# Group normalisation of 128 images: the loads of scale and offset move from SP's DMA queue to ACT's

## Chip, cores and metric

The kernel runs on one core of a Trainium2 chip. The metric is the device time of one execution in microseconds, lower being better. The time before is the median of three runs.

## The reference

```python
# x: (128, 1024, 32, 16), g and b: (1024,), all bfloat16
def reference(x, g, b):
    G = 32
    B, C, H, W = x.shape
    xr = x.reshape(B, G, C // G, H, W)
    mu = xr.mean(axis=(2, 3, 4), keepdims=True)
    var = ((xr - mu) ** 2).mean(axis=(2, 3, 4), keepdims=True)
    xn = (xr - mu) / jnp.sqrt(var + 1e-5)
    xn = xn.reshape(B, C, H, W)
    return xn * g[None, :, None, None] + b[None, :, None, None]
```

Each of 128 x 32 groups (32 channels of 512 elements, 16384 values) is normalised by its own mean and variance, and each channel is then scaled by g and shifted by b.

## The kernel before

One partition holds one group: a tile is 4 images x 32 groups = 128 partitions with 16384 bfloat16 values each, 4 MB. There are 32 tiles (NT) in 6 buffers (SLOTS). A tile is loaded into its buffer, worked on in place and stored from it.

Everything is in hand-written order with semaphores; no scheduler moves anything. Each engine has its own list of instructions.

- **SP** issues the loads (`load`, L136 to L140) on its DMA queue. Before load i it waits until the store that last used the buffer has landed, so the first six loads go without a wait, and load 6 waits for store 0. Between load 0 and load 1 it issues the loads of scale and offset (L151, L152) into `gam_b` and `bet_b`, 128 partitions with 32 values of 2 bytes. The access pattern of their source, `four`, repeats the 32 rows of g or b four times: its outer dimension is 4 with step 0. Both loads count up the semaphore `s_gb`.
- **PE** sums 16 blocks of 512 columns of the tile into PSUM with the unit matrix as weights (`sums`, L198).
- **ACT** loads its function table and runs a small square root to warm up (L182). Per tile it computes the sum of squares in two parts (`squares`, L222), then issues the store of the tile before (`stored()`, in the end L143 and L144), then waits for DVE's variance (L231) and takes the square root (L232). The first store also waits until load 3 has landed (L344). All stores are on ACT's DMA queue.
- **DVE** sets two constants, then waits for both loads of scale and offset (L183) and converts them to float32 (L184, L185). Per tile (`normalise`) it sums the rest of the columns (L243), adds PE's sums (L253), forms the mean (L263), the deviation of the shift used in the squares (L272), waits for ACT's squares (L281), forms the variance (L285), waits for ACT's root, takes the reciprocal (L294), forms the 32 scales and offsets (L296, L300) and scales the tile in place, one instruction of 512 columns for each of 32 channels (L310).
- **POOL** prepares the unit matrix.

Of the kernel before, what the change touches and what calls it, by code (L numbers as in the profile page):

```python
# [24 lines left out]
def kernel(  # L25
# [37 lines left out]
    g_v = g.rearrange("(q k) -> q k", q=G)  # L63
    b_v = b.rearrange("(q k) -> q k", q=G)
# [5 lines left out]
    def sb(name, shape, dtype):  # L70
        return ctx.enter_context(nc.sbuf_tensor(name, shape, dtype))
# [3 lines left out]
    def sem(name):  # L75
        all_sems.append(nc.alloc_semaphore(name))
        return all_sems[-1]
# [7 lines left out]
    gam_b = sb("gam_b", [P, KC], BF16)  # L85
    bet_b = sb("bet_b", [P, KC], BF16)
# [38 lines left out]
    s_gb = sem("gb")  # L125
# [8 lines left out]
    sp, pe, act, dve, pool = nc.sync, nc.tensor, nc.scalar, nc.vector, nc.gpsimd  # L134

    def load(i):  # L136
        j, n = (i + FIRST) % SLOTS, i // SLOTS
        if n > 0:
            sp.wait_ge(s_store[j], 16 * n)
        sp.dma_start(out=xs[j][:], in_=x_v[i]).then_inc(s_load[j], 16)  # L140
# [5 lines left out]
    def four(v):  # L146
        return bass.AP(tensor=v.tensor, offset=v.offset, ap=[[0, NS]] + list(v.ap))


    load(0)  # L150
    sp.dma_start(out=gam_b[:], in_=four(g_v)).then_inc(s_gb, 16)  # L151
    sp.dma_start(out=bet_b[:], in_=four(b_v)).then_inc(s_gb, 16)  # L152
    for i in range(1, NT):
        load(i)
    for j in range(SLOTS):
# [7 lines left out]
        out=half[:],  # L163
        in_=ones[:],
# [8 lines left out]
        out=eye[:],  # L173
        in_=half[:],
# [3 lines left out]
        base=0,  # L178
        channel_multiplier=-1,
    ).then_inc(s_eye, 1)  # L180
    act.wait_ge(s_eps, 1)
    act.activation(out=warm[:], in_=eps_t[:], func=ACT.Sqrt)  # L182
    dve.wait_ge(s_gb, 32)  # L183
# [7 lines left out]
        out=ps[0][:, 0:P], lhsT=eye[:], rhs=eye[:], start=True, stop=True  # L191
# [215 lines left out]
```

## Time and profile before

| | before |
|---|---|
| median of three runs | 630.02 us (629.59 to 630.5) |
| the profiled execution | 630.21 us |
| its span | 628.5 us |
| DVE busy | 539.9 us (86%) |
| ACT busy | 471.2 us (75%) |
| PE busy | 185.0 us (29%) |
| moved by DMA | 268.48 MB, 427 GB/s on average |
| SP's DMA queue (q1) | 4872 packets, 134.24 MB |
| ACT's DMA queue (q10) | 4608 packets, 134.22 MB |

The span is the profiled execution from its first to its last instruction; the device time is 1.7 us longer. Busy times are of one engine; the engines work side by side. The two DMA queues are lists that the same 16 DMA engines work off. The page counts packets, one contiguous piece of a transfer each: 32 KB for a partition of x, 64 bytes for a partition of scale or offset, 4 bytes for the write to a semaphore that ends an engine's share of a transfer.

### The profile page before, as it was taken

What the parts mean: (1) busy time and instruction counts of PE and PEld (TensorE: products, weight loads), DVE (VectorE), ACT (ScalarE), POOL (GpSimd) and SP (SyncE); (2) the same over time, 40 slices, a digit from 0 to 9 for tenths busy, and PEclk for the clock granted to TensorE, in tenths of its full rate; (3) what the DMA queues carried; (4) which work ended last, traced back from release to release, by engine and by line L of the source; (5) the groups of instructions that cost most, each with busy time, mean ns of one, the idle gap of its engine ahead of it and who ended that gap; (6) DMA issues with size and microseconds to landing.
All of it is one profiled execution on the core that took longest, in us unless ns stands there. A gap on an engine that the chain in (4) does not pass through costs nothing.

```text
span 628.5 us, 2380 instructions
## 1 busy us (share of the span) xinstructions
PE 185.0 (29%) x508; PEld 0.1 (0%) x1; DVE 539.9 (86%) x1380; ACT 471.2 (75%) x162; POOL 0.8 (0%) x6
## 2 busy tenths in 40 slices
PE   1655214321333312343113332133330234312300
PEld 0000000000000000000000000000000000000000
DVE  0587999999999999999999988889888898888970
ACT  2977888888889888888879777797676886768800
POOL 0000000000000000000000000000000000000000
PEclk9767666656676567666666766677656766566655
DMA  9999999999999999999999999999999999999997
GB/s 368 429 434 422 428 411 434 434 434 434 432 434 434 434 434 434 430 434 434 432 434 434 432 434 434 434 434 432 432 434 434 434 432 430 432 432 434 432 434 309
DMA packets 9483, 268.48 MB, mean 427 GB/s; under 512 B 1288, under 2 KB 1288, under 8 KB 1288
## 3 DMA queue, kind: packets, MB, share of 16 engines
q1 hardware_dynamic: 4872, 134.24, 49.8%
q10 hardware_dynamic: 4608, 134.22, 49.5%
q14 instruction: 3, 0.02, 0.0%
HBM read 134.23 MB, written 134.22 MB: 427 GB/s over the span
## 4 chain that ended last, share of the span: by engine, by line
another core or an unknown queue 42%; DVE 30%; DMA 18%; SPq 2%; issue 2%; ACT 2%; ACTq 1%; DVEq 0%
DVE x L310 20%; DMA x<-in_x_dram 10%; DMA out_dram<-x 8%; DVE jp L243 7%; SPq L140 2%; ACT js L222 1%; DVE jd L253 1%; ACTq L144 1%; ACT scalars L232 1%; DVE bia L300 1%; DVE scl L296 0%; DVE scalars L285 0%; DVE scalars L263 0%; DVE scalars L272 0%
## 5 line engine op out<-in xcount | busy, mean ns | idle before, releaser
L222 ACT ACTIVATE js<-x 128x8192 uint8<-128x8192 bf16 x64 | 455.6, 7119 | 69.6 <-DMA x<-in_x_dram 67.9
L310 DVE TENSOR_SCALAR x<-x,scl,bia 128x512 bf16<-128x512 bf16 x1024 | 333.6, 406 | 1.2
L198 PE MATMUL ps<-x,eye 128*128 128x512 bf16 x507 | 184.7, 541 | 402.6 <-DMA x<-in_x_dram 401.5
L243 DVE SCALAR_TENSOR_TENSOR jp<-x 128x4096 uint8<-128x4096 bf16 x32 | 141.3, 4416 | 1.1 <-issue 1.1
L232 ACT ACTIVATE scalars<-scalars,eps_t 128x1 f32<-128x1 f32 x32 | 9.4, 294 | 56.7 <-DVE scalars L285 49.5
L281 DVE TENSOR_TENSOR scalars<-scalars 128x1 f32<-128x1 f32 x32 | 4.9, 154 | 32.1 <-ACT js L222 32.0
L253 DVE TENSOR_SCALAR_CACHE_REDUCE jd<-ps 128x512 f32<-128x512 f32 x32 | 22.2, 693 | 0.0
L294 DVE RECIPROCAL scalars<-scalars 128x1 f32<-128x1 f32 x32 | 5.2, 164 | 16.0 <-ACT scalars L232 16.0
L222 ACT ACTIVATION_READ_ACCUMULATOR js<-x 128x1 f32 x64 | 11.9, 186 | 0.0
L184 DVE CAST gam<-gam_b 128x32 f32<-128x32 bf16 x1 | 0.2, 182 | 12.5 <-DMA bet_b<-in_b_dram 12.5
L300 DVE SCALAR_TENSOR_TENSOR bia<-scl,scalars,bet 128x32 f32<-128x32 f32 x32 | 8.1, 252 | 1.1
L296 DVE TENSOR_SCALAR scl<-gam,scalars 128x32 f32<-128x32 f32 x32 | 7.7, 242 | 1.1
L272 DVE TENSOR_SCALAR scalars<-x,scalars 128x1 f32<-128x1 bf16 x32 | 6.9, 214 | 1.4 <-DVE scalars L263 0.3
L285 DVE SCALAR_TENSOR_TENSOR scalars<-scalars 128x1 f32<-128x1 f32 x32 | 7.0, 219 | 1.1
L263 DVE TENSOR_SCALAR scalars<-scalars 128x1 f32<-128x1 f32 x32 | 6.9, 214 | 1.1
L253 DVE DVE_READ_ACCUMULATOR jd<-ps 128x1 f32 x32 | 4.5, 139 | 0.0
L243 DVE DVE_READ_ACCUMULATOR jp<-x 128x1 f32 x32 | 2.6, 81 | 0.0
L182 ACT ACT_TABLE_LOAD x1 | 1.3, 1283 | 1.0 <-ACTq L66 1.0
L159 DVE MEMSET eps_t<- 128x1 f32 x1 | 0.1, 59 | 1.1 <-ACTq L66 1.1
L190 PE MATMUL ps<-eye 128*128 128x128 bf16 x1 | 0.3, 287 | 2.1 <-POOL eye L172 2.1
L162 POOL TENSOR_SCALAR_AFFINE_SELECT half<-ones 128x128 bf16<-128x128 bf16 x1 | 0.3, 292 | 0.9 <-DVE ones L160 0.9
L172 POOL TENSOR_SCALAR_AFFINE_SELECT eye<-half 128x128 bf16<-128x128 bf16 x1 | 0.3, 292 | 0.1
(8 smaller groups left out, 1.0 us busy)
## 6 DMA issues: line engine op xcount, KB each, us to landing
x<-in_x_dram SPq DMA_DIRECT2D x32, 4096.0 KB, 26.3
out_dram<-x ACTq DMA_DIRECT2D x32, 4096.0 KB, 50.4
gam_b<-in_g_dram SPq DMA_DIRECT2D x1, 8.0 KB
bet_b<-in_b_dram SPq DMA_DIRECT2D x1, 8.0 KB
```

Source lines behind the costliest of these rows:

```text
L140: sp.dma_start(out=xs[j][:], in_=x_v[i]).then_inc(s_load[j], 16)
L198: m = pe.add_instruction(mybir.InstMatmult(name=nc.get_next_instruction_name(), ins=[pe.lower_ap(xs[j][:, k * MM_FREE : (k + 1) * MM_FREE] ...
L222: act.activation(out=js[:, 0 : part.shape[1]], in_=part, func=ACT.Square, bias=xs[j][:, 0:1], scale=-1.0, accum_out=sq[j][:, k : k + 1],). ...
L232: act.activation(out=std[j][:], in_=nvar[j][:], func=ACT.Sqrt, bias=eps_t[:], scale=-inv_n,).then_inc(s_std[j], 1)
L243: dve.scalar_tensor_tensor(out=jp[:], in0=xs[j][:, PE_COLS : PE_COLS + PAIRS], scalar=1.0, in1=xs[j][:, PE_COLS + PAIRS : F], op0=ALU.mult ...
L253: dve.tensor_scalar(out=jd[:], in0=ps[j][:], scalar1=1.0, scalar2=None, op0=ALU.mult, op1=ALU.add, accum_out=sum1[j][:],).then_inc(s_sums[ ...
L263: dve.tensor_scalar(out=negmean[j][:], in0=sum1[j][:], scalar1=sum2[j][:], scalar2=-inv_n, op0=ALU.add, op1=ALU.mult,).then_inc(s_mean[j], 1)
L272: dve.tensor_scalar(out=d[j][:], in0=xs[j][:, 0:1], scalar1=negmean[j][:], scalar2=float(ROOT), op0=ALU.add, op1=ALU.mult,)
L285: dve.scalar_tensor_tensor(out=nvar[j][:], in0=d[j][:], scalar=d[j][:], in1=sqsum[j][:], op0=ALU.mult, op1=ALU.subtract,).then_inc(s_nvar[ ...
L296: dve.tensor_scalar(out=scl[j][:], in0=gam[:], scalar1=rstd[j][:], scalar2=None, op0=ALU.mult).then_inc(s_scl[j], 1)
L300: dve.scalar_tensor_tensor(out=bia[j][:], in0=scl[j][:], scalar=negmean[j][:], in1=bet[:], op0=ALU.mult, op1=ALU.add,).then_inc(s_bia[j], 1)
L310: v = dve.tensor_scalar(out=xs[j][:, k * HW : (k + 1) * HW], in0=xs[j][:, k * HW : (k + 1) * HW], scalar1=scl[j][:, k : k + 1], scalar2=bi ...
```

## The change

The two DMA issues for scale and offset are taken from SP's list, where they stood between load 0 and load 1, and put on ACT's list ahead of the function table load and the warm-up. Their source, destination and semaphore stay the same, and so does every wait.

```diff
     load(0)
-    sp.dma_start(out=gam_b[:], in_=four(g_v)).then_inc(s_gb, 16)
-    sp.dma_start(out=bet_b[:], in_=four(b_v)).then_inc(s_gb, 16)
     for i in range(1, NT):
         load(i)
...
+    act.dma_start(out=gam_b[:], in_=four(g_v)).then_inc(s_gb, 16)
+    act.dma_start(out=bet_b[:], in_=four(b_v)).then_inc(s_gb, 16)
     act.wait_ge(s_eps, 1)
     act.activation(out=warm[:], in_=eps_t[:], func=ACT.Sqrt)
     dve.wait_ge(s_gb, 32)
     dve.tensor_copy(out=gam[:], in_=gam_b[:])
     dve.tensor_copy(out=bet[:], in_=bet_b[:]).then_inc(s_gbf, 1)
```

In the compiled list of ACT the two DMAs stand ahead of the table load. The lists of PE, DVE and POOL are the same as before but for line numbers.

## The prediction

> **What bounds the kernel now.** I read the page first, then the timeline of the first 62 us, the DMA answers for short windows, and the end of the chain of waits.
>
> The page says that the DMA engines are the wall:
>
> ```profile
> DMA  9999999999999999999999999999999999999997
> GB/s 368 429 434 422 428 411 434 434 434 434 432 434 434 434 434 434 430 434 434 432 434 434 432 434 434 434 434 432 432 434 434 434 432 430 432 432 434 432 434 309
> DMA packets 9483, 268.48 MB, mean 427 GB/s; under 512 B 1288, under 2 KB 1288, under 8 KB 1288
> ```
>
> Each load or store of x is 128 packets of 32 KB, 8 on each of 16 engines, and the packet records give 1.213 us for one in steady traffic: 9.70 us for 4 MB. 64 transfers make 64 x 9.70 = 621 us of the 628.5 us span, after a first packet at 2.29 us. DVE (86% busy, 17.38 us from one tile to the next: 51.09, 68.48, 85.86 in the chain) is faster than load plus store (19.4 us). So a change can cost time only by leaving DMA engines without work, and can gain only what they lose now, about 5 us.
>
> The start, from the timeline:
>
> ```profile
> 0.99 0.38 SPq L140 DMA_DIRECT2D x<-in_x_dram  x1
> 1.03 1.28 ACT L182 ACT_TABLE_LOAD   x1 [1.03 <-ACTq L66]
> ...
> 1.43 0.69 SPq L151 DMA_DIRECT2D gam_b<-in_g_dram  x1
> ...
> 2.18 0.67 SPq L152 DMA_DIRECT2D bet_b<-in_b_dram  x1
> ...
> 13.23 7.12 ACT L222 ACTIVATE js<-x 128x8192 uint8<-128x8192 bf16 x1 [10.70 <-DMA x<-in_x_dram]
> ...
> 13.79 0.18 DVE L184 CAST gam<-gam_b 128x32 f32<-128x32 bf16 x1 [12.47 <-DMA bet_b<-in_b_dram]
> ```
>
> Scale and offset are issued at 1.43 and 2.18 but land only at 13.49, behind load 0 on the same queue. How small their own work is, the DMA answer for 12.72 to 13.50 us shows:
>
> ```profile
> DMA packets 185, 0.24 MB, mean 308 GB/s; under 512 B 178, under 2 KB 178, under 8 KB 178
> q1 hardware_dynamic: 185, 0.24, 85.0%
> ```
>
> By the packet records these are 64-byte packets, 256 in all. 1288 small packets less 256, less 64 x 16 semaphore writes for x, leave 8: two transfers by 4 engines. So four engines carry 64 small packets each. Alone on an engine they follow each other every 7 ns: 0.45 us.
>
> How an engine shares itself between the two queues is seen once store 0 (ACT's queue, q10) meets load 5 (SP's, q1), from 53 to 61 us:
>
> ```profile
> q10 hardware_dynamic: 51, 1.67, 48.3%
> q1 hardware_dynamic: 48, 1.54, 44.8%
> ```
>
> 51 packets against 48, and by the records' starts and ends they alternate one for one. A turn is one packet of 1.213 us, whichever queue has the longer list.
>
> **The change, part by part.**
>
> Two DMA issues leave SP (0.69 + 0.67 + gaps = 1.52 us, 1.37 to 2.89), and load 1 could be issued at about 1.43. It gains nothing: load 0 keeps the engines busy until 12.7, and in the timeline loads 1 to 5 are all issued by 11.62.
>
> The two issues go to ACT ahead of the table load: 2 x 0.68 = 1.4 us, so the table load moves from 1.03 to about 2.5 and the warm-up ends at 3.9. ACT next works at 13.23; 9 us of cover. The trace does not show an ACT issue into four engines beside running loads. The nearest rows are SP's 0.67 us and the slowest ACT issue, store 0 with 4.99 us (L144). Two such would end the warm-up at 12.5, still covered; ACT's cost is nothing, and beyond 0.7 us more the excess would be paid.
>
> The small packets leave the head of load 1 on four engines: a gain of up to 0.45 us there, and as much back wherever else they run on the same engines. Zero.
>
> The deciding term is when they land on the new queue. They can no longer wait as one block behind load 0; they share turns with it. If one turn passes one descriptor, each 64-byte packet waits for one 32 KB packet of x. 64 of them need 64 x 1.213 = 77.6 us, but SP's queue holds only 6 loads until a store frees a slot: 6 x 8 = 48 packets per engine. After those the engine has nothing else and the rest pass at 7 ns each. Offset then lands when load 5 has drained: load 3 landed at 44.5 before, and two more at 9.70 make T = 63.7 us on the slowest engine (61.2 on the fastest). The other bound is the block itself: about 3 us if all small packets pass at once. Between these ends I take T = 63.7, because the only row with two queues on one engine shows turns of one packet.
>
> A page bears on this. The Trainium skill, DMA: Bandwidth & Descriptors, section "Queues, rings and completion order", says that an engine goes round its queues packet by packet, and that a packet there typically holds 9 to 17 descriptors. The one-for-one alternation of 32 KB pieces disagrees with that for x: a load's 8 descriptors on an engine are not one turn. By the page, estimated with 9 to 17, the small ones would need 4 to 8 turns and land before load 0; that is the first rival below.
>
> What T = 63.7 costs: DVE's first instruction after its memsets waits for both loads (L183), and all statistics and scaling on DVE are queued behind it. ACT squares tile 0 and then waits at L231 for DVE. From landing to the first packet of store 0, by rows of before:
> - landing to cast, 13.49 to 13.79: 0.30
> - cast to the first sum, 13.79 to 15.15: 1.36
> - sums to the deviation, 15.15 to 21.11: 5.96
> - square sum to offsets, 27.72 to 29.26: 1.54 (the wait for ACT from 21.1 to 27.7 falls away, the squares are long done)
> - 32 scalings: 10.43
> - end of scaling to issue, 61.52 to 61.71: 0.19
> - issue to first packet, 0.99 to 2.29: 1.30
>
> Sum 21.08 us, in which no queue holds work. Store 0's packets start at 84.8. Tile 1's second square part has been dispatched by then, so ACT's order adds nothing.
>
> Then the refill: SP's load 6 waits for store 0 to land (84.8 + 9.7 + 0.2 = 94.7) and its packets start 0.1 + 1.3 later: 1.4 to 1.6 us idle. Store 1 follows 17.38 us after store 0, and load 7 again waits for its landing (115.5): 1.6 more; a third time store 3 arrives at 137.0 where the engines ran dry at 136.5: 0.5. After that stores are always queued. Sum 3.7. Before loses something in the same phase that would not recur: 413 of 434 GB/s over 75 to 95 us (1.0) and 404 over 52.7 to 61.7 (0.6). Net 2.1 to 3.7, say 2.9.
>
> 21.1 + 2.9 = 24.0 us. Nothing takes it back: before leaves the engines dry only at the head, and after the gap DVE ends its last tile at 83.3 + 31 x 17.38 = 622, well before the engines finish store 30, so the end stays DMA's. The profiled execution took 630.21 us (span 628.5), 0.19 over the median 630.02. 630.21 + 24.0 - 0.2 = **654 us**.
>
> **The rivals.**
>
> *No change: many small descriptors pass in one turn.* For it: 4-byte semaphore writes follow the last data packet of their queue at once in the records and take no turn of their own. Against: that is one such write behind its own data, never a series. If four or more pass per turn, there are at most 16 turns, T is 3 + 19.4 = 22 or less, DVE's scaling of tile 0 ends by T + 19.6 = 42, and store 0 is not issued before load 3 lands anyway (L344; 44.96 in the row of L144). Then offset landing anywhere up to T = 25 is free. DVE's casts move from 13.79 to before load 0 lands, its first sum from 15.15 to about 13.3, and it then waits longer for ACT's squares (27.72). Time 629.8, within 629.3 to 630.4. It decides as soon as four descriptors pass a turn.
>
> *Half-way: two or three per turn.* T = 3 + 32 x 1.213 = 42 or 29. Store 0's packets start at T + 21 = 63 or 50: at 42 just after the loads ran dry, and the refill idles cost 2 to 5 us: 632 to 635; at 29 nearly nothing.
>
> *A small gain.* The slowest DMA engine writes its last semaphore at 627.11 us, the next at 626.25. If the slow one is among the four and its 64 small packets slip in while its first packet of x is still starting (those take 1.9 instead of 1.2 us), the end comes up to 0.86 us earlier: 629.2. To be faster by more than 0.2% (1.26 us, about what a measurement here can tell from no change) other losses would have to go too. Below 629 I see no mechanism.
>
> That the loads do not move is excluded: in the changed program ACT's order is the two DMAs, then the table load.
>
> **How the numbers follow.** One descriptor a turn: 0.65, with its own range of 648 to 661: below, if the first phase drains at 61.2 and the slow engine's lag is absorbed (about 652), or a few small packets pass per turn at the start; above, if each of 48 turns costs 0.1 us more on the four engines (+5). Half-way: 0.08. Another slowdown, such as a blocked table load: 0.02. No change: 0.20. Gain over 0.2%: 0.05. Likeliest and half-way hold 0.73, so a range for 8 in 10 has to take in no change as well: 629.3 to 661. Slower 0.75, same 0.20, faster 0.05.
>
> **What the profile after would show.** Right: the DVE cast (L184) starts not at 13.8 but near 64; ACT stops at L232 after the squares of tile 0; the DMA row has a hole of about 21 us after 61 us, in its fourth to sixth slice; store 0 is issued near 83; the last slices look as before. Wrong: the cast starts before 13 us, and the hole is missing; then one turn passes many descriptors and the time is 630. A cast between 25 and 45 us means a few per turn. If the cast is late and no hole follows, the queue of loads was deeper than I count. If ACT's first square starts later than 13.5, the issues on ACT were not covered.

## The result and the profile after

The changed kernel takes 657.37 us (median of five runs, 656.99 to 658.41) against 630.5 us of before (median of five runs too; the first three had 630.02): ratio 1.0422, 95% interval 1.0393 to 1.0452. Its profiled execution took 656.99 us with a span of 655.3; before it was 630.21 and 628.5. So 26.8 us have come in.

First the page of the changed kernel, the same rows as before:

```profile
DMA  9997089899999999999999999999999999999996
GB/s 376 424 436 301 1 353 416 352 448 416 448 416 448 416 446 418 446 418 446 422 442 442 422 448 416 446 418 446 418 446 418 446 422 442 434 430 448 416 446 294
...
q1 hardware_dynamic: 4608, 134.22, 47.9%
q10 hardware_dynamic: 4872, 134.24, 47.6%
```

The 264 packets of scale and offset have moved from q1 to q10. The DMA row has a hole: 301 GB/s in the fourth slice, 1 in the fifth, 353 in the sixth, and weaker slices behind it (416, 352). From then on it swings mostly between 416 and 448 about the 434 of before.

The timeline says who waits:

```profile
1.04 1.17 ACTq L179 DMA_DIRECT2D gam_b<-in_g_dram  x1
2.25 0.55 ACTq L180 DMA_DIRECT2D bet_b<-in_b_dram  x1
2.83 1.28 ACT L182 ACT_TABLE_LOAD   x1 [2.83 <-issue]
...
13.28 7.12 ACT L222 ACTIVATE js<-x 128x8192 uint8<-128x8192 bf16 x1 [8.96 <-DMA x<-in_x_dram]
...
62.39 0.18 DVE L184 CAST gam<-gam_b 128x32 f32<-128x32 bf16 x1 [61.07 <-DMA bet_b<-in_b_dram]
...
69.71 0.29 ACT L232 ACTIVATE scalars<-scalars,eps_t 128x1 f32<-128x1 f32 x1 [41.96 <-DVE scalars L285]
...
81.82 0.38 ACTq L144 DMA_DIRECT2D out_dram<-x  x1
```

The first two lines are issued at 1.04 and 2.25 us, and ACT is ready at 4.3, nine microseconds before tile 0. But DVE's cast comes at 62.39 instead of 13.79; ACT stands still for 41.96 us at its first square root; and store 0 goes out at 81.82 instead of 44.96. The kernel before has in place of the last two rows:

```profile
28.17 0.29 ACT L232 ACTIVATE scalars<-scalars,eps_t 128x1 f32<-128x1 f32 x1 [0.48 <-DVE scalars L285]
...
44.96 4.99 ACTq L144 DMA_DIRECT2D out_dram<-x  x1
```

How the two queues share the engines in between, from the DMA answer for 14 to 40 us (packets, MB, share of 16 engines):

```profile
q1 hardware_dynamic: 370, 11.08, 98.8%
q10 hardware_dynamic: 92, 0.01, 0.2%
```

92 packets in 26 us on four engines are 23 on each. In 26 us an engine passes 26 / 1.213 = 21.4 packets of x, and it ends two of x's loads, whose writes to the semaphore take a turn too. So every descriptor (one entry of a transfer's list, moved as one packet) of x, large or a 4-byte write, lets one 64-byte packet pass, no more. The packet records show it one by one: on the engine that begins first, small packets start at 6.42, 7.64, 8.86 and 10.07 us. Scale's last small packets end by 40.9 us and its writes to the semaphore by 42.1. With offset each engine gets as far as 49 of its 64 small packets; then SP's queue is empty, and the DMA answer for 61 to 62 us shows the rest pass together, 15 packets and one semaphore write on each of four engines:

```profile
DMA packets 76, 0.00 MB, mean 4 GB/s; under 512 B 76, under 2 KB 76, under 8 KB 76
q10 hardware_dynamic: 64, 0.00, 4.3%
```

What follows in the stretches after that (length; busy us and count of PE, PEld, DVE, ACT and POOL; clock, DMA share, GB/s):

```profile
61.70:82.70 21.00, 6.01 (x16) 0.00 (x0) 18.65 (x46) 12.96 (x4) 0.00 (x0) 0.58 0.01 3
82.70:92.50 9.80, 0.00 (x0) 0.00 (x0) 9.23 (x25) 6.79 (x4) 0.00 (x0) 0.50 0.99 425
92.50:94.10 1.60, 0.00 (x0) 0.00 (x0) 1.60 (x6) 1.60 (x1) 0.00 (x0) 0.50 0.00 0
```

21.0 us without a packet of x while DVE (18.65 busy) works off tile 0; store 0 alone; then 1.6 us in which no packet starts, until load 6, which had to wait for that store. In the kernel before the first of these stretches is full:

```profile
61.70:82.70 21.00, 5.97 (x15) 0.00 (x0) 20.43 (x44) 17.94 (x7) 0.00 (x0) 0.67 1.00 431
```

### The profile page after: what moved, and what is told of

Same layout as the page of the kernel before. It is cut to its first block, busy times and chain, and to the rows that moved or that the text cites. A ratio compares the mean times of both kernels' runs of the same rounds, so it can differ in the third digit from the quotient of the medians.

```text
span 655.3 us, 2385 instructions
## 1 busy us (share of the span) xinstructions
PE 182.1 (28%) x513; PEld 0.1 (0%) x1; DVE 539.2 (82%) x1380; ACT 470.6 (72%) x162; POOL 0.8 (0%) x6
## 4 chain that ended last, share of the span: by engine, by line
DVE 44%; another core or an unknown queue 36%; DMA 11%; ACT 4%; issue 2%; SPq 0%; DVEq 0%; ACTq 0%
DVE x L310 27%; DVE jp L243 11%; DMA out_dram<-x 7%; DMA x<-in_x_dram 4%; ACT js L222 3%; DVE jd L253 2%; ACT scalars L232 1%; DVE bia L300 1%; DVE scl L296 1%; DVE scalars L285 1%; DVE scalars L263 1%; DVE scalars L272 1%; DVE scalars L294 0%; SPq L140 0%
## 5 line engine op out<-in xcount | busy, mean ns | idle before, releaser
L198 PE MATMUL ps<-x,eye 128*128 128x512 bf16 x512 | 181.8, 533 | 429.9 <-DMA x<-in_x_dram 429.9
L281 DVE TENSOR_TENSOR scalars<-scalars 128x1 f32<-128x1 f32 x32 | 4.9, 152 | 13.4 <-ACT js L222 13.4
```

Of the source, the lines that this page charges most:

```text
L198: m = pe.add_instruction(mybir.InstMatmult(name=nc.get_next_instruction_name(), ins=[pe.lower_ap(xs[j][:, k * MM_FREE : (k + 1) * MM_FREE] ...
```

## The experiments

**Theory.** An engine gives each queue one descriptor a turn. 64 small packets on an engine therefore land after 64 turns of x or when SP's queue runs dry; DVE's list waits for them, no store goes out, and the engines run dry. **Rivals:** the small packets or ACT's later start cost time by themselves; the small queue gets a share by time or by bytes; or several small descriptors pass per turn. All kernels are edits of the changed kernel unless said otherwise. Each ratio is to runs of before made alongside, which spread from 629.6 to 638.0 us, so it can differ by up to 0.3% from what two medians give.

**Without the wait.**

```diff
-    dve.wait_ge(s_gb, 32)
-    dve.tensor_copy(out=gam[:], in_=gam_b[:])
-    dve.tensor_copy(out=bet[:], in_=bet_b[:]).then_inc(s_gbf, 1)
+    dve.memset(gam[:], 1.0)
+    dve.memset(bet[:], 0.0).then_inc(s_gbf, 1)
...
     pool.wait_ge(s_gone, 1)
+    pool.wait_ge(s_gb, 32)
```

> Scale and offset are still loaded on ACT's queue, but nobody waits for them before the end: DVE uses the constants 1 and 0 in their place, which leaves scale and offset out of the result. Theory (the loss is DVE's wait for packets that get one turn each): the small packets still dribble in between the packets of x until about 62 us, but DVE starts with load 0 at 13.3 us, store 0 goes out near 45 us, there is no hole in the DMA row, and the time is that of before, within 1 us. Rival (the small packets slow the DMA engines themselves, or the two issues delay ACT): the wait is gone, yet 10 us or more of the 27 stay: 640 us and up.

Measured: 632.53 us, ratio to before 1.0018 (0.9984 to 1.0052). From its timeline and its DMA answer for 14 to 40 us:

```profile
44.86 0.38 ACTq L144 DMA_DIRECT2D out_dram<-x  x1
```

```profile
q10 hardware_dynamic: 95, 0.01, 0.3%
```

The small packets dribble as before (95 against 92), the last lands at 64.5 us, and store 0 still goes out at 44.86. The wait made the loss. The median is 2.3 us above the 630.26 of before alongside, where 1 us was expected; by the ratio at most 0.5% is left, and that is not told apart from nothing.

**Waiting later.** DVE waits where scale is first used, and reads the bfloat16 rows.

```diff
-    dve.wait_ge(s_gb, 32)
-    dve.tensor_copy(out=gam[:], in_=gam_b[:])
-    dve.tensor_copy(out=bet[:], in_=bet_b[:]).then_inc(s_gbf, 1)
-    dve.wait_ge(s_gbf, 1)
...
+        dve.wait_ge(s_gb, 32)
         dve.wait_ge(s_rstd[j], n)
...
-            out=scl[j][:], in0=gam[:], scalar1=rstd[j][:], ...
+            out=scl[j][:], in0=gam_b[:], scalar1=rstd[j][:], ...
...
-            in1=bet[:],
+            in1=bet_b[:],
```

> The loads stay on ACT's queue; DVE waits for them not at its start but where they are first used, ahead of the 32 scales of a tile, and reads them as bfloat16 without the two casts. Theory: they land at 61.8 as after the change, but tile 0's statistics are done by then; what is left between landing and store 0's first packet is 0.6 + 0.5 + 10.4 + 0.2 + 1.0 = 12.7 us in place of 21.0. The hole is 12.7 us and the time about 8.3 us less than after: 649 us. Rival (the hole comes from the loads of x or from ACT, not from DVE's list): no change, 657 us.

Measured: 651.37 us, ratio 1.0304 (1.0241 to 1.0366). The stretch that is empty:

```profile
63.60:76.60 13.00, 5.99 (x15) 0.00 (x0) 12.34 (x35) 0.00 (x0) 0.00 (x0) 0.63 0.00 1
```

By the packet records the hole is 13.2 us instead of 21.0: 7.8 shorter, where 8.3 was expected. The time fell by 6.0 and not 8.3: in this trace one of the four engines drained at 63.5, not at 61.7, and that 1.8 us went on top.

**Fewer turns: sixteen engines in place of four.** Each load becomes four of 32 partitions, one for each image of the tile (NS is 4, G is 32).

```diff
-    act.dma_start(out=gam_b[:], in_=four(g_v)).then_inc(s_gb, 16)
-    act.dma_start(out=bet_b[:], in_=four(b_v)).then_inc(s_gb, 16)
+    for k in range(NS):
+        act.dma_start(out=gam_b[k * G : (k + 1) * G, :], in_=g_v).then_inc(s_gb, 16)
+    for k in range(NS):
+        act.dma_start(out=bet_b[k * G : (k + 1) * G, :], in_=b_v).then_inc(s_gb, 16)
...
-    dve.wait_ge(s_gb, 32)
+    dve.wait_ge(s_gb, 32 * NS)
```

> Still on ACT's queue, but as eight loads of 32 partitions in place of two that repeat the rows four times, so that 16 engines share the packets: 16 small packets and 8 semaphore writes an engine in place of 64 and 2. Theory (one descriptor a turn, the writes to semaphores counted): 24 turns less two or three that the semaphore writes of x give away, so the last lands about 26 us after the first: the cast near 33 us in place of 62.4, store 0 issued near 53 us, before the six loads have drained at 61.7: 630 to 633 us. Rival (what counts is that SP's queue holds something, not the number of turns): the cast stays near 62 and the time near 657.

Measured: 630.32 us, ratio 0.998 (0.9953 to 1.0007): the whole loss is gone, with both loads still on ACT's queue.

```profile
30.70 0.18 DVE L186 CAST gam<-gam_b 128x32 f32<-128x32 bf16 x1 [29.38 <-DMA bet_b<-in_b_dram]
```

The last semaphore write is 26.5 us after the first small packet, as 24 turns less two or three give; the first came at 3.8 us and not at 6.4, hence 30.7 instead of 33.

**One list instead of two.** Only scale is loaded; offset is a constant 0.

```diff
-    act.dma_start(out=bet_b[:], in_=four(b_v)).then_inc(s_gb, 16)
...
-    dve.wait_ge(s_gb, 32)
+    dve.wait_ge(s_gb, 16)
...
-    dve.tensor_copy(out=bet[:], in_=bet_b[:]).then_inc(s_gbf, 1)
+    dve.memset(bet[:], 0.0).then_inc(s_gbf, 1)
```

> Only scale is loaded, on ACT's queue; offset is left out (the constant 0 in its place), so one list of 33 descriptors an engine has only packets of x to share with. Theory: 33 turns less four that the semaphore writes of x give away, 29 x 1.213 us after the first at 6.4: lands near 41.9, as scale does after the change, cast near 42.4, store 0's first packet 20.9 us later at 62.8, about 1.1 us after the loads drain at 61.7; the two refill gaps stay. 634 to 638 us. Rival (it always lasts until SP's queue is empty): cast at 62.4, 657 us.

Measured: 637.42 us, ratio 1.0086 (1.0056 to 1.0116).

```profile
42.48 0.18 DVE L183 CAST gam<-gam_b 128x32 f32<-128x32 bf16 x1 [41.17 <-DMA gam_b<-in_g_dram]
```

Counting turns gave 41.9 us for the landing, and the semaphore writes came at 41.8 to 42.0. There is hardly a hole (1.6 us per engine between 60 and 70 us). Yet 5.4 us are lost by the ratio, 7.2 between the two profiled executions, with an empty stretch at 74.0 (1.4 us) and one at 96.5 (0.5): a late first store costs refill time even where it leaves hardly a hole.

**Offset alone on ACT's queue, scale left on SP's.**

```diff
     load(0)
+    sp.dma_start(out=gam_b[:], in_=four(g_v)).then_inc(s_gb, 16)
...
-    act.dma_start(out=gam_b[:], in_=four(g_v)).then_inc(s_gb, 16)
```

> Only the load of offset goes on ACT's queue; that of scale stays on SP's queue between load 0 and load 1. Theory (one descriptor a turn, whatever its size): offset has had some five turns by 12.4 us, when load 0 drains; then SP's queue too holds small packets, 33 descriptors an engine, and the two alternate at 7 ns each, so that offset's other 28 pass with them. The cast near 13.6 us, no hole, 630 to 631 us. Rival (turns by time or bytes, or half the packets do half the harm): offset lands near 42 us and the time is 634 to 645 us.

Measured: 630.03 us, ratio 0.998 (0.9958 to 1.0002).

```profile
14.04 0.18 DVE L184 CAST gam<-gam_b 128x32 f32<-128x32 bf16 x1 [12.72 <-DMA gam_b<-in_g_dram]
```

The DMA answer for 12.4 to 13.4 us has the rest of offset pass together, 112 packets in that microsecond:

```profile
q10 hardware_dynamic: 112, 0.01, 7.7%
```

Half of the change costs nothing, while the other experiment with one load on ACT's queue lost 5 to 7 us. The difference is what SP's queue holds: beside another list of small packets, turns take nanoseconds. A fixed share of time or bytes, such as the 0.2% of time in the 26 us above, would not do that.

**Shorter turns.** Each load and store of x becomes two of 2 MB, in the changed kernel and, as a control, in the kernel before; waits on loads and stores count 32 in place of 16.

```diff
-        sp.dma_start(out=xs[j][:], in_=x_v[i]).then_inc(s_load[j], 16)
+        for c in (0, F // 2):
+            sp.dma_start(
+                out=xs[j][:, c : c + F // 2], in_=x_v[i][:, c : c + F // 2]
+            ).then_inc(s_load[j], 16)
...
-        act.dma_start(out=o_v[i], in_=xs[j][:]).then_inc(s_store[j], 16)
+        for c in (0, F // 2):
+            act.dma_start(
+                out=o_v[i][:, c : c + F // 2], in_=xs[j][:, c : c + F // 2]
+            ).then_inc(s_store[j], 16)
```

> The changed kernel, with each load and each store of x split into two of 2 MB (left and right half of the columns): packets of 16 KB, 0.61 us each, twice as many. Theory (a turn lasts as long as one packet of the other queue): 66 turns less seven, 59 x 0.61 = 36 us after the first at 4 to 6.4: the cast near 41 to 43 us in place of 62.4, little or no hole, and 3 to 8 us over its control with the same split. Rival (the small packets get a fixed share of time or pass only when the queue is empty): cast still near 62, 25 us or more over the control.

> Control: the kernel before with the same split of loads and stores into two of 2 MB. All theories: the cast near 13.8 us and the time within 3 us of before, 629 to 633 us.

Measured: 640.42 us (ratio 1.0136, 1.0095 to 1.0177); the control 632.63 (1.0023, 1.0003 to 1.0043). The difference is 7.8 us instead of 27. From the first, the DMA answer for 14 to 40 us:

```profile
q1 hardware_dynamic: 751, 10.99, 99.5%
q10 hardware_dynamic: 185, 0.01, 0.5%
```

The same bytes of x in the same time, but twice the packets, and twice the small packets pass (185 against 92). Offset lands at 42.7 us, the cast comes at 43.20. Turns are counted in descriptors. What is left of the loss looks as with scale alone: empty stretches at 73.9 (1.4 us) and 96.7 (1.2 us).

**A gate.**

```diff
     load(0)
+    sp.wait_ge(s_gb, 32)
```

> SP waits for scale and offset before it issues load 1, so only the 8 packets per engine of load 0 compete with them. Theory: what has not had its turn passes as a block once load 0 has drained, near 12.5 us; the cast at about 13.2 us. Price: load 1 is issued only then, and the engines are dry for about 1.2 to 1.6 us. No hole at 62 us. 631 to 632.5 us. Rival (a queue of small descriptors is slow by itself, beside whatever): the cast comes well after 20 us, with the engines empty in the meantime, and the time is 640 us or more.

Measured: 632.32 us, ratio 1.0017 (0.9991 to 1.0044). Two stretches of it:

```profile
13.10:14.40 1.30, 0.99 (x3) 0.00 (x0) 0.27 (x2) 1.01 (x1) 0.00 (x0) 1.00 0.01 1
14.40:16.00 1.60, 1.60 (x6) 0.00 (x0) 1.07 (x1) 1.60 (x1) 0.00 (x0) 1.00 1.22 328
```

With load 0 alone to share with, everything has landed at 13.2 us, and the price is the gap until load 1 arrives, 1.5 us by the packet records. A queue of small descriptors is not slow by itself.

Sixteen engines and offset alone come out level with before; no version here beats it beyond its interval.

## Why the prediction was right

The forecast was 654 us, the sum of a hole of 21.1 us and a net refill of 2.9 on top of before; measured are 657.37. The mechanism held step by step, and one term was too small.

- **SP's two issues gone: no gain.** Right. All six loads are issued by 4.1 us, and it helps nobody.
- **ACT's cost: covered.** Right. Warm-up ends at 4.3 (3.9 was forecast: scale's issue took 1.17 us and not 0.68); tile 0's squares start at 13.28 against 13.23.
- **One descriptor a turn.** Right, and now shown by count, by length of turn and by the other queue's contents. The Trainium skill, DMA: Bandwidth & Descriptors, section "Queues, rings and completion order", says that a turn passes one packet of typically 9 to 17 descriptors. The 23 per engine in 26 us beside 21.4 packets of x do not agree with it. The rivals with several small packets a turn fall. So does what the first of them had in its favour, that a semaphore write takes no turn of its own: scale's last small packets end by 40.9 us, its writes start about one packet of x later, and the counts above come out only with the writes counted.
- **Four engines.** Right: the packet records have four semaphore writes for each of the two loads, and sixteen engines take the loss away. The Trainium skill, DMA: Bandwidth & Descriptors, section "Why a DMA increments its semaphore by 16 and not by 1", derives the number of engines from the slowest dimension of both patterns. The traces agree: the repeated rows (4) gave four engines and 32 partitions gave sixteen.
- **T = 63.7.** 61.8. The prediction set the packet records 0.3 us late against the instructions (load 0's first packet is at 1.99, the small ones end at 13.19), and the engine that trailed load 3 before did not trail here. The sum does not change with it, since it counts from T.
- **The sum of 21.08.** The hole is 20.99. From landing to cast 0.57 and from issue to first packet 0.88 were put at 0.30 and 1.30, mostly the same 0.3 twice. Store 0 was issued 0.59 after the last scaling and not 0.19, but the sums took 5.52 to the deviation and not 5.96. That the total fits to 0.1 us is in part luck: these errors cancel.
- **Refill, net 2.9.** This term was too small; 26.8 less 21.0 leaves 5.8. Of the three idles that were forecast two are there (empty from 92.7 to 94.1 and from 115.9 to 117.0) and the third, 0.5, did not come. Counted engine by engine the idle time from 60 to 120 us is 25.1 us: 21.5 for the hole, since most engines ran dry a little before the last, and 3.6 for the two gaps, 1.8 each, against 3.7 for three. So the idle time was sized well. What failed is the step behind it, that before's losses in this phase "would not recur" and 1.6 may be taken off. Long packets come again: summed over the whole execution, what packets of x take beyond 1.213 us is 4.0 us per engine after the change and 2.4 before. At 94.1 and 117.0 the first packet on each engine takes 1.5 to 2.1 us (behind the gate above, at 328 GB/s, 1.8 to 2.2), and between 100.7 and 104.4, with no gap ahead of them, others take up to 1.95. The first packets of store 0, behind the hole itself, take only 1.21 to 1.33, so a pause alone does not make them long; what does was not tried. 25.1 and 1.5 more make 26.6 of the 26.8. The end adds up to 0.3: one engine trails the others by 2.75 us there (0.86 before), so that on average an engine's last write comes 4.3 us before the end of the span and not 4.0.

Without the subtraction the sum would have been 24.8 and the forecast 654.8 us.

## What to carry to other kernels

In this kernel a small load on a queue of its own was not ahead of the big ones: each of its descriptors waited for one packet of the other queue, until that queue was empty. So before moving such a load, count its descriptors per engine and multiply by the length of the other queue's packet (64 x 1.213 us here, cut short when the six loads had drained). Behind one big transfer on the same queue it paid for that transfer once. A first dimension that repeats rows put all descriptors on four engines; spread over sixteen, the same rows landed in half the time and cost nothing.

## What the runs showed that was not expected

After the change the first small packet moved at 6.4 us, 5.4 us after its issue, behind three packets of x on its engine; with the loads of 32 partitions it moved at 3.8, behind one. And in the kernel before two issues took very long, load 1 (5.98 us on SP) and store 0 (4.99 us on ACT), which after the change took 0.4 us each. For SP the traces have an order, which no experiment tried: count the descriptors that SP had already issued to one of the four engines, the semaphore writes included. The first load that took long (3.7 to 6.0 us) had 75 before it in the kernel before, 78 with offset alone, and 81 and 84 in the two kernels with half transfers; no load with 72 or fewer before it took over 0.7 us. Store 0 had nothing before it on ACT's queue, so this order does not explain it. What makes an issue slow stays open.
